# One core: a search for routing with one matmul per round less, transposes in threes, and a first expert in split halves, planned anew

## The chip, the core and the metric

The kernel runs on one core of a Trainium2 chip. The metric is device time in microseconds (us). A core has TensorE (matmuls; PE in the rows, and PEld for its weight loads), VectorE (DVE), ScalarE (ACT), GpSimd (POOL) and SyncE (SP); they run independently and wait for each other by semaphores. The working memory SBUF and the accumulation memory PSUM have 128 partitions; TensorE writes to PSUM only.

## The reference

Two parts. The first is a linear attention with a complex decay: for each of 4 x 8 heads and 768 positions, a state of 48 x 48 is multiplied by a normalised complex number per feature, the outer product of `k` and `v` is added to its real part, and `q` reads it.

```python
for t in range(S):
    new_re = ar * S_re - ai * S_im
    new_im = ar * S_im + ai * S_re
    S_re, S_im = (new_re + kv, new_im)
    y[:, :, t] = np.einsum('bhd,bhde->bhe', q[:, :, t], S_re)
```

The second is a mixture of eight experts with a capacity, on the 3072 tokens of 384 features that the first part gives.

```python
logits = x @ w_gate
order = np.argsort(-logits.flatten())
for idx in order:
    tok, e = (int(idx) // E, int(idx) % E)
    if assigned[tok] >= 0 or counts[e] >= cap:
        continue
    assigned[tok] = e
    counts[e] += 1
for e in range(E):
    mask = assigned == e
    out[mask] = np.maximum(x[mask] @ w1[e], 0.0) @ w2[e]
```

Each expert gets exactly 384 tokens, has a hidden width of 1024, and its weights are 384 x 1024 and 1024 x 384, all in fp32.

## The kernel before

**Attention** takes the first 223 us. It works on 24 chunks of 128 tokens; every engine has a part in it. GpSimd also builds the constants of the search there (`Router.masks`, `levels`, `level`, one call of `level` for each of five step sizes in `GRID`), between copies `gc` and `f` that attention needs.

**Routing** finds the experts one after another: whichever expert would be full first when tokens are taken in the order of their logits is settled, its tokens are taken out, and the rest is ranked again. `Router.find` does it by five rounds for each of the first seven experts. A round compares all keys with 32 thresholds (`ind`, VectorE), counts per expert how many keys are above each (`cnt`, six matmuls of bf16 on TensorE with `oh`), and moves the thresholds. As four columns of tokens go into one matmul, the counts come as four blocks, which have to be added: ScalarE copies the blocks into one column of a tile (`gather`, `comp`, four small ACTIVATEs), one matmul with the 0/1 matrix `sel` adds them, and VectorE subtracts what is needed (`cs`). VectorE then compares with zero and counts over the free axis (`f`, `fm`). Two matmuls add to the thresholds in PSUM (`thr`): one with `steps`, which needs no result, and one with `weight` and `fm`, which is the outcome of the round. The first search counts in another way (`by_pe`): 24 matmuls of which only one block is used.

From the outcome come the expert's number (`eidx`) and, by `slots`, the list of its 384 tokens (`idx`). GpSimd then starts the transfers of the expert's weights (`w1t`, `w2t`, 1.5 MB each) and of its tokens' rows (`xg`, three gathers). `update` ranks the rest.

**Experts.** `tokens` transposes the rows by nine fp32 matmuls of 128 x 128 (`acc<-ident,xg`). For experts 1 to 7 every fp32 factor is split into a high half, rounded by ScalarE (`w1h`, `xh`, `hh`, `w2h`), and the rest, taken by VectorE (`w1l`, `xl`, `hl`, `w2l`); a product is then three matmuls of 384 columns (`product`). Expert 0 (`WHOLE1`, `WHOLE2`) has no halves: one fp32 matmul a product, which stands as two records in the trace (`acc<-xh,w1t`, `acc<-w2t,hh`). There are 24 products in each of the two layers. Results are collected in five PSUM buffers named `acc`; a buffer of the first layer comes free when `hh` and `hl` have been made of it. Until the first expert's rows are there, `WARM` matmuls of constants keep TensorE running (`acc<-ident,mask`).

**The order** of everything from routing on is made by a planner on the host: `Plan` records the operations with a cost each, `rank` gives due times, moved by kind with the numbers in `M_OFF`, and `in_order` lists them for each engine. The engines run that list in order, so what waits at the head of an engine's queue holds up all that stands behind it. Nearly all instructions show line 135 (in the changed kernel 136), that of the helper that issues them, so rows are told apart by their tiles.

Of the kernel before, what the change touches and what calls it, by code (L numbers as in the profile page):

```python
# [37 lines left out]
SHUT = 8192.0  # L38
LEAD_R = 8
# [138 lines left out]
def in_order(ops, step, hop, wait, done_, start, slack, late=None):  # L178
# [25 lines left out]
    while len(done) < len(ops):  # L204
        pick = None
        for e, xs in ready.items():
            if xs:
                t = max(free[e], min(o.at for o in xs))
                o = min((o for o in xs if o.at <= t), key=lambda o: (o.prio, o.at, o.n))
                if slack and e == "dve":  # L210
                    h = min((o for o in xs if o.at <= t + 1.0), key=lambda o: (o.prio, o.at, o.n))
                    if h.prio < o.prio - 1500.0:
                        o = min((o for o in xs if o.at <= t and t + o.cost <= h.at + (0.05 if h.kind == "first" else slack)),
                                key=lambda o: (o.prio, o.at, o.n), default=h)
                t = max(t, o.at)
                if pick is None or t < pick[0]:
                    pick = t, o
        t, o = pick
        ready[o.eng].remove(o)
        cost = o.cost  # L220
        if o.eng == "pe":
            if not late_:
                cost = clock.take(t, cost, 0.84 if o.kind == "MX" else 1.0)
            elif o.main and t - busy > 3.4:
                cold = t
            if late_ and t < cold + 4.0:
                cost += min(cost, (cold + 4.0 - t) / 2)
            if o.main and side and t < run + 0.1:
                cost += BURST
            side, run = not o.main, t + cost  # L230
# [450 lines left out]
class Router:  # L681
# [27 lines left out]
    def levels(self, nc):  # L709
# [12 lines left out]
        jf = t("jf", [2, 32])  # L722
        g.iota(jf, pattern=[[1, 32]], base=0, channel_multiplier=0, allow_small_or_imprecise_dtypes=True)
        row = t("row", [2, 1])
        g.iota(row, pattern=[[0, 1]], base=0, channel_multiplier=1, allow_small_or_imprecise_dtypes=True)
        sa, sb = t("sa", [2, 32]), t("sb", [2, 32])
# [7 lines left out]
        for x in self.wide.values():  # L734
            for y in x:
                g.memset(y, 0.0)
        self.sel = t("sel", [128, 128], F16)
# [15 lines left out]
    def level(self, nc, i):  # L753
        v = g = nc.gpsimd
        jf, row, sa, sb = self.row
        d = GRID[i]
        nxt = GRID[i + 1] if i + 1 < len(GRID) else 0.0
        v.tensor_scalar(sa, jf, 1.0, -d, op0=OP.add, op1=OP.mult)
        v.tensor_scalar(sb, jf, nxt, None, op0=OP.mult)
        v.tensor_tensor(sb, sb, sa, op=OP.subtract)  # L760
        v.tensor_scalar(sb, sb, row, None, op0=OP.mult)
        v.tensor_tensor(self.steps[:2, i], sb, sa, op=OP.add)
        g.memset(self.weight[:, i], d)

    def start_plan(self, plan, wk, ps):
# [4 lines left out]
        self.wide = {n: [plan.wrap(y, BF if n == "f" else F32) for y in x] for n, x in self.wide.items()}  # L770

# [50 lines left out]
    def find(self, parts, by_pe, more):  # L822
# [16 lines left out]
        for it in range(len(GRID)):  # L839
# [131 lines left out]
    def update(self, more):  # L971
# [19 lines left out]
        v.scalar_tensor_tensor(need, e2, SHUT, cc, op0=OP.mult, op1=OP.subtract)  # L991
# [225 lines left out]
class Lane:  # L1217
# [3 lines left out]
    def __getattr__(self, name):  # L1221
        def call(*a, **k):
# [7 lines left out]
            else:  # L1230
# [3 lines left out]
                cost = n / rate / (2 if half else 1) + base  # L1234
                if self.e == "vector" and ("accum_out" in k or any(x.shape[1:] == [1] for x in ins[1:])):
                    cost += 0.06
# [26 lines left out]
def experts(nc, tc, z, router, w1, w2, xd, out):  # L1263
# [51 lines left out]
    def route(e):  # L1315
# [10 lines left out]
        rows(w1t.rearrange("p a f -> p (a f)"), w1, eidx, 128 * 3 * FF * 4, "w1d")  # L1326
        def second():
            w2t[e] = wp.tile([128, FK, DM], F32, name="w2t", bufs=2)
            rows(w2t[e].rearrange("p a f -> p (a f)"), w2, eidx, 128 * FK * DM * 4, "w2d")
# [6 lines left out]
        for j in range(3):  # L1336
            rows(xg[:, j], xd, i[:, j:j + 1], 128 * DM * 4, "xd")
# [9 lines left out]
        for kk in range(3) if e not in WHOLE1 else ():  # L1347
            split(w1t[:, kk], *(w[:, kk] for w in w1s[e]), "w1s", g if (e, kk) in W1_POOL else v)
# [7 lines left out]
    def tokens(e, xg):  # L1356
        xs = pair([128, 3, CAP], "x", 1) if e not in WHOLE1 else wp.tile([128, 3, CAP], F32R, name="xh", bufs=1)
        for kk in range(3):
            xp = pm.tile([128, 3, 128], F32, name="acc", bufs=5)
            for j in range(3):  # L1360
                o = plan.tensor.transpose(xp[:, j], xg[:, j, kk * 128:kk * 128 + 128], z.ident)
                o.main, o.kind = True, "tp"
            if e in WHOLE1:
                act(xs[:, kk].bitcast(F32), xp.rearrange("p a b -> p (a b)"), AF.Copy).kind = "x"
            else:
                split(xp.rearrange("p a b -> p (a b)"), *(x[:, kk] for x in xs), "x")
# [9 lines left out]
    for e in range(E):  # L1376
# [5 lines left out]
        for f in range(FK):  # L1382
# [6 lines left out]
            if whole2:  # L1389
                act(hs[:, f].bitcast(F32), hp, AF.Relu).kind = "h"  # L1390
                continue
            hi, lo = (h[:, f] for h in hs)
            act(hi, hp, AF.Relu).kind = "h"
            v.scalar_tensor_tensor(lo, hp, 0.0, hi.bitcast(F32), op0=OP.max, op1=OP.subtract).kind = "h"
            split(w2t[e][:, f], *(w[:, f] for w in w2s), "w2s", g if f in W2_POOL.get(e, ()) else v)
        for j in range(3):
# [7 lines left out]
            act(ot, op, AF.Copy).kind = "ot"  # L1404
# [7 lines left out]
            move(issue, [], [ot, idx[e][:, j:j + 1]], 128 * DM * 4, "out")  # L1412
# [17 lines left out]
M_STEP, M_HOP, M_WAIT, M_DONE, BURST = 0.11, 0.15, 0.56, 0.95, 0.0  # L1430
M_LATE = 0.0
M_OFF = {'find1': 835.4, 'find2': 177.3, 'find3': 5742.5, 'find4': 586.4, 'find5': 202.8, 'find6': -166.9, 'find7': 3964.4, 'first': 798.4, 'h': -267.8, 'mm': -1978.5, 'next0': -350.6, 'next1': 1725.6, 'next2': -434.0, 'next3': 1723.0, 'next4': 4459.0, 'next5': 3249.1, 'next6': 3238.8, 'ot': 399.1, 'out': 4151.6, 'slot1': 2379.8, 'slot2': 3913.1, 'slot3': 8365.8, 'slot4': -48.4, 'slot5': 45.4, 'slot6': 3905.5, 'slot7': 2159.9, 'tp': -5582.0, 'w1d': 5858.6, 'w1s': -1579.2, 'w2d': 1875.2, 'w2s': -466.1, 'warm': 426.7, 'x': 659.3, 'xd': 4044.8}
# [8 lines left out]
WHOLE1 = (0,)  # L1441
WHOLE2 = (0,)
# [49 lines left out]
```

## Time and profile before

| | |
|---|---|
| median of three timed runs | 499.46 us (499.0 to 499.57) |
| the profiled execution | 500.43 us, of which its span is 498.6 us |
| PE busy | 444.0 us (89%), 3644 matmuls |
| VectorE busy | 389.0 us (78%) |
| ScalarE busy | 305.6 us (61%) |
| GpSimd busy | 140.9 us (28%) |
| TensorE's granted clock, mean | 0.976 of full speed |

The rows that follow further down are in us from the start of the span. In the order of time each row has the start, how long it lasted, the engine, the operation with what it writes and reads, and how many follow each other (x6). Matmuls are pipelined: the duration of a row overlaps with its successors, and what one costs in a stream is the distance from start to start. A busy TensorE can therefore be slower than it has to be.

### The profile page before, as it was taken

To read this page: it belongs to the slowest core of one execution; us is meant where nothing else is said; L and a number is where in the kernel's file an instruction comes from. 1 tells how busy PE (TensorE), PEld (TensorE's weight loads), DVE (VectorE), ACT (ScalarE), POOL (GpSimd) and SP (SyncE) were. 2 spreads that over 40 slices of the span, in tenths; PEclk is the share of its full clock that TensorE was granted. 3 is DMA by queue.
4 is the path that set the end of the run, shared out by engine and by line. 5 is a ranking of instruction groups with operands and counts; after the bars stand their busy time and mean duration, and the time that the engine had idled before them with its cause. 6 is when DMAs were issued, how large, how long until landed. Compare 5 with 4: busy or idle time off the path is not lost.

```text
span 498.6 us, 9821 instructions
## 1 busy us (share of the span) xinstructions
PE 444.0 (89%) x3644; PEld 382.3 (77%) x3644; DVE 389.0 (78%) x1005; ACT 305.6 (61%) x577; POOL 140.9 (28%) x227
## 2 busy tenths in 40 slices
PE   0019999999999999995589999999999999999996
PEld 0006888888798998984465578888988888999995
DVE  5999999999999999736736878598996968925150
ACT  6999898989799859520033836374472843733241
POOL 5893020303031302121211314150321513830102
PEclk9999999999999999995599999999999999999999
DMA  7807876877897674620343415380360715650001
GB/s 236 333 11 208 269 242 214 263 228 236 265 302 182 224 199 128 186 63 34 143 158 141 177 50 173 143 307 10 96 255 32 286 49 224 267 175 16 33 16 49
DMA packets 37200, 82.52 MB, mean 165 GB/s; under 512 B 4352, under 2 KB 29184, under 8 KB 34080
## 3 DMA queue, kind: packets, MB, share of 16 engines
q1 hardware_dynamic: 29216, 41.96, 27.4%
q0 software_dynamic: 6848, 38.95, 21.3%
q10 hardware_dynamic: 1088, 0.98, 0.6%
q8 instruction: 29, 0.48, 0.4%
q14 instruction: 19, 0.16, 0.1%
HBM read 53.49 MB, written 9.44 MB: 126 GB/s over the span
## 4 chain that ended last, share of the span: by engine, by line
PE 71%; issue 14%; ACT 6%; DVE 3%; DMA 3%; POOL 2%; POOLq 1%; ACTq 0%; DVEq 0%
PE acc L135 29%; PE sc L135 14%; PE y L135 8%; PE U L135 8%; PE xp L135 4%; PE cnt L135 3%; PE kp L135 3%; ACT s L135 2%; DMA w1t<-in_w,eidx 2%; POOL out L135 2%; DMA ai<-in_a_im 1%; ACT L276 1%; ACT p L135 1%; DVE ind L135 1%; DVE f L135 1%
## 5 line engine op out<-in xcount | busy, mean ns | idle before, releaser
L135 ACT ACTIVATE hh<-acc 128x384 fp32r<-128x384 f32 (+1 forms) x64 | 31.3, 490 | 62.0 <-PE acc L135 54.1
L135 PE MATMUL sc<-mask,f 128*128 128x512 bf16 x111 | 29.3, 412 | 35.5 <-DVE f L135 35.5
L135 ACT ACTIVATE comp<-cnt 32x8 f16<-32x8 f32 (+1 forms) x144 | 24.2, 168 | 57.7 <-PE cnt L135 50.8
L135 PE MATMUL acc<-w2l,hh 128*128 128x384 f32 x168 | 56.7, 350 | 0.0
L135 PE MATMUL acc<-w2h,hl 128*128 128x384 f32 x168 | 56.3, 349 | 0.0
L135 PE MATMUL acc<-w2h,hh 128*128 128x384 f32 x168 | 55.3, 346 | 0.0
L135 PE MATMUL acc<-xh,w1h 128*128 128x384 f32 x168 | 55.1, 347 | 0.0
L135 PE MATMUL acc<-xh,w1l 128*128 128x384 f32 x168 | 54.8, 347 | 0.0
L135 PE MATMUL acc<-xl,w1h 128*128 128x384 f32 x168 | 54.5, 345 | 0.0
L135 POOL DMA_INDIRECT out<-ot,idx x24 | 24.3, 1012 | 106.5 <-ACT ot L135 97.0
L135 PEld LDWEIGHTS <-f 128*128 128x128 bf16 x111 | 10.8, 105 | 49.1 <-DVE f L135 35.5
L135 PE MATMUL sc<-KQ 96*128 96x128 f32 x384 | 48.1, 277 | 0.0
L135 DVE SCALAR_TENSOR_TENSOR hl<-acc,hh 128x384 fp32r<-128x384 f32 x56 | 30.6, 552 | 19.6 <-ACT hh L135 18.7
L135 PEld LDWEIGHTS sc<-KQ 96*128 96x128 f32 x384 | 45.1, 192 | 0.8 <-issue 0.7
L135 DVE TENSOR_TENSOR f<-kq,CS 128x1536 f32<-128x1536 f32 x24 | 41.6, 1750 | 1.0 <-ACT CS L135 0.5
L135 DVE TENSOR_TENSOR ind<-m,thr 128x768 bf16<-128x768 f32 (+1 forms) x45 | 33.9, 771 | 8.4 <-PE thr L135 8.4
L135 POOL DMA_DIRECT2D xd<-x x22 | 13.3, 604 | 93.6 <-ACT x L135 93.6
L135 POOL DMA_INDIRECT xg<-xd,idx x24 | 30.2, 1259 | 32.2 <-DVE idx L135 12.0
L135 DVE TENSOR_TENSOR am<-sc,mask 128x512 f32<-128x512 f32 x48 | 31.9, 680 | 6.8 <-PE sc L135 6.3
L135 PE MATMUL y<-am,V 128*64 128x128 f32 x384 | 36.5, 278 | 0.0
L135 PEld LDWEIGHTS acc<-w2l,hh 128*128 128x128 f32 x168 | 31.5, 189 | 0.7
L135 PEld LDWEIGHTS acc<-w2h,hl 128*128 128x128 f32 x168 | 31.3, 189 | 0.6 <-issue 0.3
(207 smaller groups left out, 1173.3 us busy)
## 6 DMA issues: line engine op xcount, KB each, us to landing
KQ<-f SPq DMA_DIRECT2D x144, 128.5 KB, 2.7
kq<-in_kq SPq DMA_DIRECT2D x8, 1152.0 KB, 6.8
V<-in_v SPq DMA_DIRECT2D x8, 576.0 KB, 5.3
xd<-x POOLq DMA_DIRECT2D x22, 192.0 KB
ar<-in_a_re SPq DMA_DIRECT2D x6, 576.0 KB, 4.1
ai<-in_a_im SPq DMA_DIRECT2D x6, 576.0 KB, 5.4
ar<-in_a_re SPq DMA_DIRECT2D x2, 384.0 KB, 4.8
ar<-in_a_re SPq DMA_DIRECT2D x2, 192.0 KB, 4.2
```

Of the source, the lines that this page charges most:

```text
L135: r = f(*a, **k)
L276: real.scalar.add_instruction(ins)
```

## The change

Five things are changed, all from routing on, but for constants that GpSimd builds in attention.

1. The rounds of `find` that are not `by_pe` (searches for experts 1 to 6, 30 rounds). ScalarE copies the four blocks to four slices of a tile `parts`, whose fifth slice holds the negated need, and one reduction on VectorE adds the five. The matmul with `sel` and the tile `comp` are gone here (the list in `slots` still uses them).
2. In the same rounds the `steps` matmul is merged into that with `fm`: the tile `fm` has ones in two spare rows (64 and 65), and `both` has the step there and the level in rows 0 to 31.
3. The three transposes of one block of features are one entry of the plan for experts 1 to 7, so they stand together.
4. `WHOLE1` and `WHOLE2` are empty: expert 0 is split like the others.
5. The planner has a cost `BURST` of 0.1 for a product behind a small matmul or a transpose, a floor for ScalarE's cost, kinds by expert, and new numbers in `M_OFF`.

```diff
-            nc.tensor.matmul(thr, z.onesb.to_broadcast([128, 128]), self.steps[:, it], start=False, stop=False, skip_group_check=True)
             if by_pe:
+                nc.tensor.matmul(thr, z.onesb.to_broadcast([128, 128]), self.steps[:, it], start=False, stop=False, skip_group_check=True)
                 nc.ops[-1].deps.append(counted)
...
             else:
-                nc.tensor.matmul(both[:, 1, :E], self.sel, self.gather(both, E), start=True, stop=True)
-                v.tensor_tensor(cnt, both[:32, 1, :E], need[:32], op=OP.subtract)
+                with nc.one():
+                    for c in range(4):
+                        nc.scalar.activation(self.parts[:, c], both[32 * c:32 * c + 32, 0, E * c:E * c + E], AF.Copy)
+                v.tensor_reduce(cnt, self.parts.rearrange("p c e -> p e c"), op=OP.add, axis=AX.X)
...
-            nc.tensor.matmul(thr, self.weight[:, it].to_broadcast([128, 128]), wide["fm"].bitcast(BF)[:, 1:2].to_broadcast([128, 32]),
-                             start=False, stop=(it == len(GRID) - 1), skip_group_check=True)
+            fmb = wide["fm"].bitcast(BF)[:, 1:2]
+            pair = (self.weight[:, it].to_broadcast([128, 128]), fmb.to_broadcast([128, 32])) if by_pe else (
+                fmb.to_broadcast([128, 128]), self.both[:, it])
+            nc.tensor.matmul(thr, *pair, start=False, stop=(it == len(GRID) - 1), skip_group_check=True)
...
-        v.scalar_tensor_tensor(need, e2, SHUT, cc, op0=OP.mult, op1=OP.subtract)
+        v.scalar_tensor_tensor(self.parts[:, 4], e2[:32], -SHUT, cc[:32], op0=OP.mult, op1=OP.add)
...
-        v.tensor_tensor(self.steps[:2, i], sb, sa, op=OP.add)
-        g.memset(self.weight[:, i], d)
+        g.tensor_tensor(self.both[r, i], sb, sa, op=OP.add)
+        g.tensor_copy(self.steps[r, i], self.both[r, i])
+        g.memset(self.both[:32, i], d)
+        g.memset(self.weight[:, i], 0.0)
+        g.memset(self.weight[:32, i], d)
...
-            for j in range(3):
-                o = plan.tensor.transpose(xp[:, j], xg[:, j, kk * 128:kk * 128 + 128], z.ident)
-                o.main, o.kind = True, "tp"
+            with plan.one() if e else nullcontext():
+                for j in range(3):
+                    o = plan.tensor.transpose(xp[:, j], xg[:, j, kk * 128:kk * 128 + 128], z.ident)
+                    o.main, o.kind = True, f"tp{e}"
...
-M_STEP, M_HOP, M_WAIT, M_DONE, BURST = 0.11, 0.15, 0.56, 0.95, 0.0
+M_STEP, M_HOP, M_WAIT, M_DONE, BURST = 0.11, 0.15, 0.56, 0.95, 0.1
...
-WHOLE1 = (0,)
-WHOLE2 = (0,)
+WHOLE1 = ()
+WHOLE2 = ()
```

**Where instructions stand.** TensorE, in the first expert: one round of the search for expert 1, from the last count (`cnt<-oh,ind`) to the outcome (`thr<-...fm`). Before:

```order
L135 LDWEIGHTS ind_2922
L135 MATMUL cnt<-oh,ind_2922 128x32
L135 LDWEIGHTS onesb
L135 MATMUL thr<-steps,onesb 128x32
L135 MATMUL acc<-xh,w1t 128x384 x2
L135 LDWEIGHTS sel
L135 MATMUL cnt<-comp_2935,sel 128x8
L135 MATMUL acc<-xh,w1t 128x384
L135 LDWEIGHTS weight
L135 MATMUL thr<-fm_183,weight 128x32
L135 MATMUL acc<-xh,w1t 128x384 x2
```

and now:

```order
L136 LDWEIGHTS ind_2920
L136 MATMUL cnt<-oh,ind_2920 128x32
L136 MATMUL acc<-xh,w1l 128x384
L136 MATMUL acc<-xl,w1h 128x384 x2
L136 MATMUL acc<-xh,w1h 128x384 x2
L136 MATMUL acc<-xh,w1l 128x384 x2
L136 MATMUL acc<-xl,w1h 128x384 x2
L136 LDWEIGHTS fm_184
L136 MATMUL thr<-both,fm_184 128x32
L136 MATMUL acc<-xh,w1h 128x384 x2
```

Between the counts and the outcome stand products alone, and the first expert's are of split halves.

VectorE, the same search for expert 1, rounds two to four (`cs` and `f,fm` are a round's outcome, `ind` the next comparison). Before:

```order
L135 TENSOR_TENSOR cs_187<-cnt,need 32x8
L135 TENSOR_SCALAR f_185,fm_183<-cs_187 32x8
L135 TENSOR_TENSOR ind_2883<-m,thr 128x768
L135 TENSOR_TENSOR cs_186<-cnt,need 32x8
L135 TENSOR_SCALAR f_184,fm_182<-cs_186 32x8
L135 TENSOR_TENSOR ind_2922<-m,thr 128x768
L135 TENSOR_TENSOR cs_187<-cnt,need 32x8
```

and now:

```order
L136 TENSOR_TENSOR w1l<-w1t,w1h 128x1024 x2
L136 TENSOR_REDUCE cs_189<-parts 32x8
L136 TENSOR_SCALAR f_187,fm_185<-cs_189 32x8
L136 TENSOR_TENSOR w1l<-w1t,w1h 128x1024
L136 TENSOR_TENSOR ind_2920<-m,thr 128x768
L136 TENSOR_TENSOR xl<-acc,xh 128x384 x3
L136 TENSOR_REDUCE cs_188<-parts 32x8
L136 TENSOR_SCALAR f_186,fm_184<-cs_188 32x8
L136 TENSOR_TENSOR ind_2957<-m,thr 128x768
L136 SCALAR_TENSOR_TENSOR hl<-acc,hh 128x384 x2
L136 TENSOR_REDUCE cs_189<-parts 32x8
```

The first expert's rests `w1l`, `xl` and `hl` stand between the steps of the search, where nothing stood.

TensorE, the transposes of expert 4's tokens among the second layer of expert 3. Before:

```order
L135 MATMUL acc<-ident,xg 128x128
L135 MATMUL acc<-w2h,hh 128x384
L135 MATMUL acc<-ident,xg 128x128
L135 MATMUL acc<-w2l,hh 128x384
L135 LDWEIGHTS weight
L135 MATMUL thr<-fm_183,weight 128x32
L135 MATMUL acc<-ident,xg 128x128
L135 MATMUL acc<-w2h,hl 128x384
L135 MATMUL acc<-ident,xg 128x128 x3
L135 MATMUL acc<-w2h,hh 128x384
```

and now, for expert 3's tokens:

```order
L136 MATMUL acc<-ident,xg 128x128 x3
L136 LDWEIGHTS fm_185
L136 MATMUL thr<-both,fm_185 128x32
L136 MATMUL acc<-w2l,hh 128x384
L136 MATMUL acc<-ident,xg 128x128 x3
L136 MATMUL acc<-w2h,hl 128x384
L136 MATMUL acc<-ident,xg 128x128 x3
```

The single transposes between products have become groups of three.

## Rows read from the trace of the kernel before

**Rows 1.** Stretches of 20 us: busy us of each engine (instructions), clock, DMA share.

```profile
240.00:260.00 20.00, 14.44 (x116) 11.50 (x116) 10.09 (x48) 4.43 (x20) 4.88 (x5) 0.76 0.54 188
260.00:280.00 20.00, 20.00 (x95) 11.58 (x94) 13.42 (x65) 9.41 (x27) 4.76 (x5) 1.00 0.48 187
380.00:400.00 20.00, 19.74 (x131) 17.59 (x130) 18.43 (x77) 12.02 (x35) 6.50 (x7) 1.00 0.54 202
```

**Rows 2.** PE in order of time: start, duration, operation.

```profile
296.95 0.33 PE L135 MATMUL acc<-xl,w1h 128*128 128x384 f32 x1
...
298.51 0.34 PE L135 MATMUL acc<-xl,w1h 128*128 128x384 f32 x1
...
298.99 0.34 PE L135 MATMUL acc<-xh,w1h 128*128 128x384 f32 x1
```

**Rows 3.** PE in order of time, first expert and start of the second.

```profile
255.61 0.91 PE L135 MATMUL acc<-xh,w1t 128*128 128x384 f32 x2 [0.35 <-ACT xh L135]
...
266.86 4.76 PE L135 MATMUL acc<-xh,w1t 128*128 128x384 f32 x14
271.45 0.42 PE L135 MATMUL cnt<-rh,o 128*128 128x96 bf16 x6
...
287.84 0.63 PE L135 MATMUL acc<-xh,w1h 128*128 128x384 f32 x1
```

**Rows 4.** PE in order of time, around small matmuls of the search for expert 3.

```profile
305.55 0.34 PE L135 MATMUL acc<-w2l,hh 128*128 128x384 f32 x1
...
306.02 0.33 PE L135 MATMUL acc<-w2h,hl 128*128 128x384 f32 x1
...
308.62 0.18 PE L135 MATMUL thr<-steps,onesb 128*128 128x32 bf16 x1
308.65 0.42 PE L135 MATMUL acc<-w2h,hh 128*128 128x384 f32 x1
...
309.25 0.33 PE L135 MATMUL acc<-w2h,hh 128*128 128x384 f32 x1
...
309.91 0.34 PE L135 MATMUL acc<-w2l,hh 128*128 128x384 f32 x1
```

**Rows 5.** PE in order of time, around transposes alone and in three.

```profile
315.17 0.27 PE L135 MATMUL acc<-ident,xg 128*128 128x128 f32 x1
...
315.46 0.27 PE L135 MATMUL acc<-ident,xg 128*128 128x128 f32 x1
...
378.31 0.49 PE L135 MATMUL acc<-ident,xg 128*128 128x128 f32 x3
378.56 0.42 PE L135 MATMUL acc<-w2h,hh 128*128 128x384 f32 x1
```

**Rows 6.** Three engines in order of time, one round of a search, and its list.

```profile
257.76 0.30 PE L135 MATMUL cnt<-oh,ind 128*128 128x32 bf16 x6
258.16 0.71 ACT L135 ACTIVATE comp<-cnt 32x8 f16<-32x8 f32 x4 [1.84 <-PE thr L135]
259.55 0.15 DVE L135 TENSOR_TENSOR cs<-cnt,need 32x8 f32<-32x8 f32 x1 [2.00 <-PE cnt L135]
260.07 0.18 PE L135 MATMUL thr<-fm,weight 128*128 128x32 bf16 x1
...
273.84 0.17 DVE L135 CAST idx<-at 128x3 int32<-128x3 f32 x1
```

**Rows 7.** VectorE's groups: times, busy us, mean ns of one, idle before.

```profile
L135 DVE SCALAR_TENSOR_TENSOR hl<-acc,hh 128x384 fp32r<-128x384 f32 x56 | 30.6, 552 | 19.6 <-ACT hh L135 18.7
L135 DVE TENSOR_TENSOR w2l<-w2t,w2h 128x384 fp32r<-128x384 f32 x56 | 29.0, 547 | 0.0
L135 DVE TENSOR_TENSOR w1l<-w1t,w1h 128x1024 fp32r<-128x1024 f32 x21 | 25.1, 1213 | 0.8 <-ACT w1h L135 0.8
```

**Rows 8.** GpSimd and VectorE in order of time, early in attention.

```profile
29.79 0.58 POOL L135 COPY f<-gc 128x6 f32<-128x6 f32 x2
33.65 5.20 DVE L135 TENSOR_TENSOR f<-kq,CS 128x1536 f32<-128x1536 f32 x3 [0.38 <-ACT CS L135]
```

More of the change, by code (lines that the diff above doesn't have):

```diff
@@ L1 @@
 import math
-from contextlib import ExitStack, contextmanager
+from contextlib import ExitStack, contextmanager, nullcontext
 import concourse.bass as bass
@@ L38 @@
 SHUT = 8192.0
+STEP_ROW = 64
 LEAD_R = 8
@@ L227, in in_order @@
                 cost += min(cost, (cold + 4.0 - t) / 2)
-            if o.main and side and t < run + 0.1:
+            small = not o.main or o.kind.startswith(("tp", "warm"))
+            if side and not small and t < run + 0.1:
                 cost += BURST
-            side, run = not o.main, t + cost
+            side, run = small, t + cost
             if o.main:
@@ L736, in levels @@
                 g.memset(y, 0.0)
+        for y in self.wide["fm"]:
+            g.memset(y[STEP_ROW:STEP_ROW + 2], 1.0)
+        self.parts = t("parts", [32, 5, E])
         self.sel = t("sel", [128, 128], F16)
@@ L753, in level @@
     def level(self, nc, i):
-        v = g = nc.gpsimd
-        jf, row, sa, sb = self.row
+        g = nc.gpsimd
+        r = slice(STEP_ROW, STEP_ROW + 2)
+        jf, row, sa, sb = (x[r] for x in self.row)
         d = GRID[i]
         nxt = GRID[i + 1] if i + 1 < len(GRID) else 0.0
[L758 to L761, printed above, removed]
-        v.tensor_tensor(self.steps[:2, i], sb, sa, op=OP.add)
-        g.memset(self.weight[:, i], d)
+        g.tensor_scalar(sa, jf, 1.0, -d, op0=OP.add, op1=OP.mult)
+        g.tensor_scalar(sb, jf, nxt, None, op0=OP.mult)
+        g.tensor_tensor(sb, sb, sa, op=OP.subtract)
+        g.tensor_scalar(sb, sb, row, None, op0=OP.mult)
+        g.tensor_tensor(self.both[r, i], sb, sa, op=OP.add)
[3 more added lines that the diff above has]
+        g.memset(self.weight[:32, i], d)
     def start_plan(self, plan, wk, ps):
@@ L770, in start_plan @@
         self.wide = {n: [plan.wrap(y, BF if n == "f" else F32) for y in x] for n, x in self.wide.items()}
+        self.parts = plan.wrap(self.parts)
     def mine(self, n, shape, dt=F32):
@@ L1234, in call @@
                 cost = n / rate / (2 if half else 1) + base
+                if self.e == "scalar":
+                    cost = max(cost, 0.18)
                 if self.e == "vector" and ("accum_out" in k or any(x.shape[1:] == [1] for x in ins[1:])):
@@ L1336, in route @@
         for j in range(3):
-            rows(xg[:, j], xd, i[:, j:j + 1], 128 * DM * 4, "xd")
+            rows(xg[:, j], xd, i[:, j:j + 1], 128 * DM * 4, f"xd{e}")
         if e in W2_LATE:
@@ L1347, in route @@
         for kk in range(3) if e not in WHOLE1 else ():
-            split(w1t[:, kk], *(w[:, kk] for w in w1s[e]), "w1s", g if (e, kk) in W1_POOL else v)
+            split(w1t[:, kk], *(w[:, kk] for w in w1s[e]), f"w1s{e}", g if (e, kk) in W1_POOL else v)
         plan.kind = f"next{e}"
@@ L1389, in experts @@
             if whole2:
-                act(hs[:, f].bitcast(F32), hp, AF.Relu).kind = "h"
+                act(hs[:, f].bitcast(F32), hp, AF.Relu).kind = f"h{e}"
                 continue
             hi, lo = (h[:, f] for h in hs)
-            act(hi, hp, AF.Relu).kind = "h"
-            v.scalar_tensor_tensor(lo, hp, 0.0, hi.bitcast(F32), op0=OP.max, op1=OP.subtract).kind = "h"
-            split(w2t[e][:, f], *(w[:, f] for w in w2s), "w2s", g if f in W2_POOL.get(e, ()) else v)
+            act(hi, hp, AF.Relu).kind = f"h{e}"
+            v.scalar_tensor_tensor(lo, hp, 0.0, hi.bitcast(F32), op0=OP.max, op1=OP.subtract).kind = f"h{e}"
+            split(w2t[e][:, f], *(w[:, f] for w in w2s), f"w2s{e}", g if f in W2_POOL.get(e, ()) else v)
         for j in range(3):
@@ L1411, in issue @@
                 scat.append(s)
-            move(issue, [], [ot, idx[e][:, j:j + 1]], 128 * DM * 4, "out")
+            move(issue, [], [ot, idx[e][:, j:j + 1]], 128 * DM * 4, f"out{e}")
             if j == 2 and e == E - 2:
```

22 lines of the change are left out of this document (12 added, 10 removed).

## The prediction

> **What bounds the kernel now.** I read the stretches first. From 260 us on TensorE is busy for 20.00 of 20 us in one stretch and 19.74 in another [rows 1], so the experts are bound by what TensorE issues, and each start that disappears from its queue is time off the end. VectorE beside it rises from 13.42 to 18.43 us of 20: a second engine that is not far from its own limit. Only in 240 to 260 us is TensorE not full (14.44 busy, granted clock 0.76, a mix of the levels 1.2 and 2.4 GHz) and VectorE half idle (10.09). Attention before that keeps its instructions on every engine but GpSimd.
>
> Then TensorE in order of time. In an undisturbed run nine products of 128x384 start between 296.95 and 298.51, so one takes 0.173 us [rows 2]. The 0.33 us that each row shows as duration overlaps with the next; what counts is the distance of the starts. The first expert's unsplit fp32 products cost two records each: fourteen records stand between 266.86 and 271.45, 0.328 each, 0.656 a product [rows 3].
>
> **Search rounds.** A small matmul in the stream costs more than its own turn, because the product behind it is followed late. Around a lone `sel` the starts go from 305.55 to 306.02, 0.47 for two products that alone take 0.35: 0.12 us. Where `sel` also waits for ScalarE's copy, 309.25 to 309.91, it is 0.31 [rows 4]. About one place in four is of the second kind, so I take 0.17. The `steps` matmul costs 0.03 (308.62 to 308.65) right behind the counts, and 0.48 less 0.35, 0.13, where it stands alone (298.51 to 298.99) [rows 2, 4]. Only seven of them stand alone in the order behind the first product; I take 0.05. The change removes both from each of 30 rounds. Ten rounds lie in the first expert's stretch, treated below as a whole. The 20 of the searches for experts 3 to 6 stand in a full stream: 20 x 0.22 = **-4.4 us**. The ends are 20 x 0.15 = 3.0 and 20 x 0.44 = 8.8. VectorE's subtraction becomes a sum over five parts on the same engine, and ScalarE still makes four copies; both cost nothing, since they take the place of an equal one.
>
> The Trainium skill, "TensorE: Matmul & The Clock Gate", section "Wait — 56ns, not 53.3ns?", has a floor of about 25 ns between starts, however small the matmul; two of them in 20 rounds would then bring an estimated 1.0 us instead of 4.4, and the result would be 3.4 us later. The start behind the small one agrees with that page (0.03), but the one after it comes late, and there the trace decides.
>
> **Grouped transposes.** Alone between products a transpose costs 315.17 to 315.46, 0.29 less 0.17: 0.12 us, three of them 0.36. Three in a row occupy 378.31 to 378.56, 0.25, and the product behind is followed 0.09 late: 0.34 [rows 5, 4]. Twenty-one groups of three thus gain at most 21 x 0.02 = 0.4 us. Many stood in runs already, so I take **-0.1**.
>
> **First expert.** Its 48 products at 0.656 (31.5 us) become 144 at 0.173 (24.9): -6.6 us of TensorE [rows 2, 3]. TensorE could also start earlier. Its first product now waits until 255.61 for `xh`, which stands behind a round's copies on ScalarE; in the new order `xh` comes before them, so I put the start at 254.1: -1.5.
>
> Both are kept only if the inputs of the next expert come earlier too. These are late results of the search for expert 1, whose list of tokens is ready at 273.84 [rows 6]; from there come the row gathers, the transposes and, at 287.84, its first product [rows 3]. VectorE carries this search, and the change puts in front of that list three `w1l` of 1.213, three `xl` and seven `hl` of about 0.55, and eight `w2l` of 0.547: 3.6 + 5.5 + 4.4 = 13.5 us [rows 7]. It had 9.9 + 6.6 us idle in the two stretches [rows 1], but in waits between rounds. The bounds are therefore 0 (all of it falls into waits) and +13.5 (none does). Walking both queues by hand with the durations of the rows, I find the list at about 276.9 instead of 273.84, 3 us later in spite of shorter rounds, and expert 1's first product at about 285.3 instead of 287.84. At that point the order leaves 23 split products of the first expert (4.0 us), where before five fp32 products were left (3.3 us). So the whole first stretch, its ten rounds included, is worth -2.5 + 0.7 = **-1.8 us**; in it TensorE stands still for some 4.5 us, at the closing counts and ranks of the search and longest, 1.6 us, at the counts of the list. The ends are -10.3 (6.6 + 1.5 + 10 x 0.22, no stall) and +3.2 (13.5 less 10.3, no cover at all).
>
> **Replanned order.** From a round's counts to its `fm` matmul something must happen that no order shortens: 257.76 to 258.16 until ScalarE starts, 0.71 for four copies, some 0.1 to VectorE, and 259.55 to 260.07 from there to `fm` [rows 6]: 1.7 us, ten products. The new order leaves 8 to 12 products there, where the old one had the time of `sel` as well. I add **+1.0** for such waits over the 20 rounds; 0 and +10 are the ends (below).
>
> **GpSimd** gets three more small instructions in each of the five levels and a few fills. Behind three levels stand its two copies into `f` for chunks 1 and 2, from 29.79 for 0.58 us; the stacking that reads them also waits for VectorE's rotation, which fills those tiles from 33.65 for 5.20 us [rows 8]. Chunk 1's turn ends at about 37.1. The nine instructions ahead of the copies have some 6.8 us before they are late, so I cost them at nothing; what they took above that would be added to the start of attention.
>
> **Sum.** -1.8 - 4.4 - 0.1 + 1.0 = -5.3 against the profiled execution: its own time is 500.43 (span 498.6 and what lies around it), so 495.1. The three timed runs have their median at 499.46, 0.97 lower, and I move the forecast by as much: **494.2 us**.
>
> **Rivals.** *No stall in the first expert.* If VectorE's extra work falls into its waits, the first stretch gives 10.3 instead of 1.8: about 485.7. For it: 16.5 us idle against 13.5 [rows 1, 7]. Against: the search runs on the same queue, in order. Chance 0.10.
>
> *The clock comes late.* The granted clock was 0.76 over 240 to 260 us [rows 1]: for some 9.6 us of it TensorE was at 1.2 GHz and rose while it ran multiplications of constants without pause. The new order mixes transposes into these, which wait for gathered rows. If TensorE is at 1.2 GHz for 6 us more, products take 0.35 instead of 0.17 there, and 3 us are lost: 497. Chance 0.10. The same page of the Trainium skill, section "Part 4: PE-mode transpose", says that transposes do not count as busy for the clock; by that rule this rival is the likely one. The old order ran nine transposes behind its warm-up and reached the higher level all the same, so the trace bears it out only in part.
>
> *Accumulators run out* (slower). Five `acc` buffers hold products until VectorE has made `hl`. In the new order only one or two of an expert's eight `hl` stand ahead of the next search's ranking; the rest come behind it. TensorE covers 5 x 9 x 0.173 = 7.8 us. If VectorE needs over that between freeing two buffers, TensorE stops in each expert: at 18.43 of 20 us busy [rows 1] there is little to give. A loss of 2 us in experts 1 to 5 each is +10: 504. It decides from about 1.1 us each, where the 5.3 are gone. Chance 0.12.
>
> *The rounds bring nothing.* If the search chain, not the number of starts, sets when TensorE goes on, the 4.4 us turn into waits at `fm`, and only the first stretch is left: 499, no difference. Against it: TensorE shows no wait of note behind 260 us. Chance 0.06.
>
> **Numbers.** The forecast case has 0.62, with 490 to 497 as its own range. Faster by over 0.2% (1.0 us, about what a measurement of this kernel can tell from no change): 0.62 + 0.10 + 0.10 = 0.82. Same 0.06. Slower 0.12. The range 487.5 to 499.0 leaves out the slower rival and most of the case without a stall, under 2 in 10.
>
> **What would show it.** Right: no `steps` or `sel` matmul in rounds; the first product of the first expert near 254 and expert 1's near 285; TensorE idle for about 4 us between 262 and 285, put down to VectorE; a period of about one us less for each of experts 2 to 5. Wrong: a granted clock below 1.00 after 256 us; waits of TensorE on `hl` in every expert; waits on `fm` that add up to several us; or a first expert without idle time.

## The result, and the profile after it

The changed kernel takes 492.17 us (median of four runs, 491.21 to 493.07) against 499.25 (four runs, 499.0 to 499.57): a ratio of 0.9853, with a 95% interval of 0.9835 to 0.9872. It is faster, as forecast, and 2.0 us faster than the 494.2 of the forecast. Two more groups of runs in the experiments give 492.36 against 498.91 and 493.75 against 500.0, 6.2 to 6.6 us apart instead of 7.1.

The profiled execution took 491.21 us with a span of 489.4, so it is 9.2 us below that of before (498.6) and the fastest of all runs of the changed kernel. The terms below are read from this pair. It overstates the gain: the profiled execution of before lay 1.2 us above the median of its four runs, that of the changed kernel 1.0 below. The other runs of the changed kernel lie 0.8 to 3 us above it, and not always for one reason: of the two that were profiled too (`again` and `again2`, below), one has its first routing matmul at 228.94 instead of 226.56, the other loses 1.3 us behind 291 us, half of it in a wait for ScalarE's copy `ot`.

The stretches of 20 us, with the columns of [rows 1]:

```profile
240.00:260.00 20.00, 14.06 (x124) 12.61 (x125) 16.56 (x65) 7.40 (x23) 5.91 (x5) 0.77 0.52 188
260.00:280.00 20.00, 18.82 (x126) 16.02 (x124) 17.85 (x80) 10.49 (x35) 4.91 (x6) 1.00 0.44 177
380.00:400.00 20.00, 20.00 (x145) 18.08 (x144) 17.02 (x43) 14.36 (x46) 4.42 (x5) 1.00 0.47 190
```

VectorE has 4.4 to 6.5 us more in the two stretches of the first expert, and TensorE is no longer full in the second: 18.82 instead of 20.00. Behind that TensorE is full again.

TensorE in order of time, as [rows 3] and [rows 5]: the first routing matmul, the first product, the counts of the list, the next expert's first product, and the last one of all:

```profile
226.56 0.19 PE L136 MATMUL thr<-start,onesb 128*128 128x32 bf16 x1 [0.98 <-ACT x L136]
...
254.68 0.44 PE L136 MATMUL acc<-xh,w1h 128*128 128x384 f32 x1 [0.36 <-ACT xh L136]
...
273.12 0.43 PE L136 MATMUL cnt<-rh,o 128*128 128x96 bf16 x6 [0.99 <-DVE rh L136]
...
283.42 0.44 PE L136 MATMUL acc<-xh,w1h 128*128 128x384 f32 x1
...
484.26 0.34 PE L136 MATMUL acc<-w2h,hl 128*128 128x384 f32 x1
```

In the kernel before, the last product stands at 493.48 and the first routing matmul at 224.96:

```profile
224.96 0.19 PE L135 MATMUL thr<-start,onesb 128*128 128x32 bf16 x1 [0.97 <-ACT x L135]
```

So routing began 1.60 us **later** than before (226.56 to 224.96), and the first product came 0.93 earlier all the same (255.61 [rows 3] to 254.68): routing itself took 2.5 us less. Of these, 2.35 lie between the issue of the first row gather and the first product: 9.12 us before (246.49 to 255.61), 6.77 now (247.91 to 254.68).

The waits of TensorE's matmuls from 253 us to the end, so with the last transposes ahead of the first product, by engine and what it waited for: us, times, longest.

```profile
PE cnt L136 <- DVE rh L136: 1.0, 1, 1.0
PE acc L136 <- ACT xh L136: 0.4, 1, 0.4
PE acc L136 <- DMA xg<-xd,idx: 0.3, 1, 0.3
PE cnt L136 <- DVE ind L136: 0.2, 1, 0.2
```

Only one is above 0.4 us, and none is on `hl` or `fm`. But a matmul also waits through the load of its weights, and for `fm` and for a buffer that `hl` sets free it does so there:

```profile
PEld L136 <- DVE f L136: 2.4, 11, 0.4
PEld acc L136 <- DVE hl L136: 1.1, 4, 0.4
```

These are small: the load for a small matmul stands 0.16 us idle at almost every place, whatever it waits for, and only three of the eleven are above that (0.45, 0.43 and 0.25). The four for `hl` are 0.38, 0.29, 0.26 and 0.19.

A round of the search for expert 3, from the outcome to the next counts and the outcome after that:

```profile
302.26 0.34 PE L136 MATMUL acc<-xh,w1l 128*128 128x384 f32 x1
302.44 0.19 PE L136 MATMUL thr<-both,fm 128*128 128x32 bf16 x1
302.48 0.42 PE L136 MATMUL acc<-w2l,hh 128*128 128x384 f32 x1
302.74 0.34 PE L136 MATMUL acc<-xl,w1h 128*128 128x384 f32 x1
...
303.78 0.32 PE L136 MATMUL cnt<-oh,ind 128*128 128x32 bf16 x6
303.95 0.60 PE L136 MATMUL acc<-w2h,hl 128*128 128x384 f32 x2
```

Between 302.26 and 302.74 lie two products, 0.35 us, and the outcome, which costs 0.13 as before. Neither `sel` nor `steps` stands in the round any more: that is two matmuls less per round, not the one of the title.

**The ledger.** From the starts of all matmuls between the first product and the last I took off 0.1736 us for each of the products of 128x384 (the distance of starts in runs of products alone, 0.173 to 0.174) and 0.656 for each unsplit one. What is left is small matmuls and waits. I cut it where the search for expert 2 closes (its `thr<-start`, 293.89 before and 291.18 after).

| part, in the profiled executions | forecast | measured |
|---|---|---|
| attention, up to the first routing matmul | 0 | +1.6 |
| routing, to the first product | -1.5 | -2.5 |
| first expert: 48 x 0.656 = 31.5 to 144 x 0.1736 = 25.0 | -6.6 | -6.5 |
| small matmuls and waits up to the cut: 5.4 to 8.9 | +6.3 | +3.5 |
| the same behind the cut: 26.2 to 20.9 | -3.5 | -5.3 |
| sum | -5.3 | -9.2 |

(The forecast's first stretch was -1.8; with -1.5 and -6.6 in it, +6.3 was left for small matmuls and waits. Its -3.5 is -4.4 - 0.1 + 1.0.)

### The profile page after: what moved, and what is told of

Its sections match the earlier page's. It is cut to its first block, busy times and chain, and to the rows that moved or that the text cites. A ratio compares the mean times of both kernels' runs of the same rounds, so it can differ in the third digit from the quotient of the medians.

```text
span 489.4 us, 9869 instructions
## 1 busy us (share of the span) xinstructions
PE 431.8 (88%) x3632; PEld 386.0 (79%) x3632; DVE 401.4 (82%) x1027; ACT 311.4 (64%) x588; POOL 141.1 (29%) x245
## 4 chain that ended last, share of the span: by engine, by line
PE 66%; issue 12%; POOL 6%; DVE 5%; DMA 5%; ACT 3%; SPq 2%; POOLq 1%; ACTq 0%; DVEq 0%
PE acc L136 27%; PE sc L136 12%; PE y L136 8%; PE U L136 7%; PE xp L136 4%; PE cnt L136 3%; DMA w1t<-in_w,eidx 3%; PE kp L136 3%; SPq L136 2%; POOL sb L136 2%; DMA pick<-in_w_gate 1%; ACT w1h L136 1%; DVE ind L136 1%; POOL sel L136 1%; POOL out L136 1%
## 5 line engine op out<-in xcount | busy, mean ns | idle before, releaser
L136 PE MATMUL acc<-xh,w1h 128*128 128x384 f32 x192 | 62.5, 344 | 0.4 <-ACT xh L136 0.4
L136 PE MATMUL acc<-xh,w1l 128*128 128x384 f32 x192 | 62.0, 341 | 0.0
L136 PE MATMUL acc<-xl,w1h 128*128 128x384 f32 x192 | 61.7, 341 | 0.0
L136 PE MATMUL acc<-w2h,hl 128*128 128x384 f32 x192 | 61.4, 344 | 0.0
L136 PE MATMUL acc<-w2h,hh 128*128 128x384 f32 x192 | 61.3, 344 | 0.0
L136 ACT ACTIVATE hh<-acc 128x384 fp32r<-128x384 f32 x64 | 30.2, 492 | 35.9 <-PE acc L136 35.5
L136 ACT ACTIVATE parts<-cnt 32x8 f32<-32x8 f32 x120 | 20.1, 168 | 44.2 <-PE cnt L136 41.7
L136 PEld LDWEIGHTS acc<-xh,w1h 128*128 128x128 f32 x192 | 35.6, 189 | 1.8 <-DVE hl L136 0.8
L136 PEld LDWEIGHTS acc<-xl,w1h 128*128 128x128 f32 x192 | 35.8, 189 | 0.2
L136 PEld LDWEIGHTS acc<-w2h,hh 128*128 128x128 f32 x192 | 35.6, 188 | 0.4 <-DVE hl L136 0.3
```

Of the source, the lines that this page charges most:

```text
L136: r = f(*a, **k)
```

## Why attention starts later

ScalarE and GpSimd in order of time, near 30 us, in the kernel before (ScalarE, then GpSimd):

```profile
28.95 1.28 ACT L276 ACT_TABLE_LOAD   x1
30.25 1.16 ACT L135 ACTIVATE s<-ai 128x1152 f32<-128x1152 f32 x1
```

```profile
29.44 0.29 POOL L135 COPY gc<-s 128x6 f32<-128x6 f32 x1
```

and in the changed kernel:

```profile
28.27 1.28 ACT L278 ACT_TABLE_LOAD   x1
32.31 1.16 ACT L136 ACTIVATE s<-ai 128x1152 f32<-128x1152 f32 x1 [2.76 <-POOL gc L136]
```

```profile
20.07 1.42 POOL L136 TENSOR_SCALAR sb<-jf 2x32 f32<-2x32 f32 x1
...
29.74 0.33 POOL L136 TENSOR_SCALAR sb<-jf 2x32 f32<-2x32 f32 x1
...
32.09 0.19 POOL L136 COPY gc<-s 128x6 f32<-128x6 f32 x1
```

ScalarE's square writes into a tile that GpSimd's copy `gc` must have read. Before, `gc` ended at 29.73, half a microsecond ahead of the end of ScalarE's table load at 30.23. Now it stands behind nine more instructions, ScalarE waits 2.76 us for it, and TensorE's first matmul of attention comes at 37.53 instead of 35.51:

```profile
35.51 4.88 PE L135 MATMUL sc<-mask,f 128*128 128x512 bf16 x11 [35.51 <-DVE f L135]
```

```profile
37.53 2.74 PE L136 MATMUL sc<-mask,f 128*128 128x512 bf16 x6 [37.53 <-DVE f L136]
```

The three levels ahead of `gc` took 12.35 us (19.74 to 32.09), and 9.91 before (19.53 to 29.44): 2.4 more. Most of that is the nine instructions themselves: from the sum `both` of the third level to `gc` are 0.93 us (31.16 to 32.09), where before the sum `steps` and `gc` lay 0.22 apart (29.22 to 29.44), so 0.7 a level.

In both kernels the levels also lasted longer than their instructions alone would. The same instruction `sb<-jf` took 0.33 us at 29.74 and 1.42 at 20.07, where VectorE ran a sum of two tiles of SBUF:

```profile
19.98 1.34 DVE L136 TENSOR_TENSOR s<-s,s 128x1152 f32<-128x1152 f32 x1
```

The Trainium skill, "SBUF — State Buffer", section "SBUF: two separate sides", says that VectorE, in an operation with two inputs in SBUF, and a GpSimd operation that reads SBUF exclude each other for a whole instruction. The rows agree: 20.07 plus 1.42 is 21.49, just behind the end of VectorE's at 21.32.

Three runs test it. In late_const only the fills and copies that nothing in attention needs were moved behind the last level:

```diff
         g.tensor_tensor(self.both[r, i], sb, sa, op=OP.add)
-        g.tensor_copy(self.steps[r, i], self.both[r, i])
-        g.memset(self.both[:32, i], d)
-        g.memset(self.weight[:, i], 0.0)
-        g.memset(self.weight[:32, i], d)
+        if i < len(GRID) - 1:
+            return
+        g.tensor_copy(self.steps[r], self.both[r])
+        g.memset(self.weight, 0.0)
+        for n, x in enumerate(GRID):
+            g.memset(self.both[:32, n], x)
+            g.memset(self.weight[:32, n], x)
```

> GpSimd builds the parts of the new constants that no step of attention needs (the copy to steps, the fills of both and weight) behind the last of the five levels instead of within each. Theory: in the changed kernel the copy gc stands behind three longer levels and holds ScalarE's square for 2.76 us, so attention starts 1.7 us late; then gc comes near 29.0 us, TensorE's first matmul near 35.5 us instead of 37.5, and the time is 490.4 us. Rival: the late start comes from transfers or the spread of the start, not from GpSimd's queue; then TensorE's first matmul stays near 37.5 us and the time near 492.2.

Beside it ran the unaltered kernel:

> The changed kernel once more, unaltered, to see how its profile and its median stand to each other. Expected: 492.2 us within 0.5, and first count matmul of attention near 37.5 us again. If the first profile (491.21) was the typical one and the three later runs were disturbed, the median comes out near 491.2.

Measured: 490.38 us (489.65 to 493.77), the unaltered kernel 492.36 (492.0 to 493.24), both against 498.91. That is 2.0 less, as the theory has it. The rows went only half the way: in the profile of late_const `gc` comes at 31.38 and not near 29.0, ScalarE still waits 0.88 for it (3.54 in the control), and TensorE's first matmul is at 36.84, the control's at 38.20. That execution is the slowest of its five, for a reason given at the end. The unaltered kernel's median is near the one of its first group, so the first profiled execution is the fastest and not the typical one.

late_all moves all that only the search needs, so also masks that the kernel before had in front of `gc`:

```diff
+    def rest_of(self, nc):
...
+        g.tensor_copy(self.steps[r], self.both[r])
...
-        parts = [self.masks, self.levels] + [lambda nc, i=i: self.level(nc, i) for i in range(len(GRID))]
+        parts = [self.masks, self.levels] + [lambda nc, i=i: self.level(nc, i) for i in range(len(GRID))] + [self.rest_of]
...
-    op(("later", n), "pool", LATER[n], NT - 1.0, lambda fn=fn: fn(nc), [("later", n - 1)])
+    op(("later", n), "pool", LATER[n], NT - 1.0, lambda fn=fn: fn(nc), [("later", n - 1)] + ([("P0", 5)] if n == 7 else []))
```

> As late_const, but everything that only the search needs (sel, the masks of the list, the fills) is built behind the copies of the third group of chunks, where GpSimd has some 25 us free. Theory: ScalarE no longer waits for gc at all (0.88 us were left in late_const, 2.8 to 3.5 in the changed kernel), TensorE's first matmul comes near 35.2 us, and the time is 489.6 us. Rival: gc is not what holds the start; then 492.3 us.

This first run had no changed kernel beside it, and came to 494.34 (493.1 to 496.11) against 500.08: not what was expected, although TensorE's first matmul was at 35.83 and the first product at 253.49. So it was repeated with a control on the same chip.

> late_all again, now beside the changed kernel on the same chip. Theory (GpSimd's longer constants hold ScalarE's square, and with it attention): 2 us less than the control, 1.5 to 2.5, TensorE's first matmul 2 us earlier. Rival (what is gained at the start is lost again behind it): within 0.7 us of the control.

> The changed kernel unaltered, as a control for the three runs beside it on the same chip: 492 to 496 us, 1.2 to 1.5% below the kernel before.

Measured: 490.72 (490.31 to 491.72) against 493.75 (492.3 to 494.15) of the control, 3.0 less; the profiles are 1.6 apart (spans 488.9 and 490.5). ScalarE in late_all_b, then in the control:

```profile
28.16 1.28 ACT L278 ACT_TABLE_LOAD   x1
29.45 1.16 ACT L136 ACTIVATE s<-ai 128x1152 f32<-128x1152 f32 x1
```

```profile
29.43 1.28 ACT L278 ACT_TABLE_LOAD   x1
31.52 1.16 ACT L136 ACTIVATE s<-ai 128x1152 f32<-128x1152 f32 x1 [0.81 <-POOL gc L136]
```

The wait is gone, and TensorE's first matmul moves from 36.74 to 34.68. Of these 2.06 us only 0.81 is the wait: ScalarE's table load came 1.27 earlier, and it varies as much in the unaltered kernel (28.27, 28.16 and 29.43 in its three profiles). Over all profiles, ScalarE waits 2.76, 3.54 and 0.81 for `gc` in the changed kernel and TensorE starts at 37.53, 38.20 and 36.74; in late_all and late_all_b it does not wait at all, and TensorE starts at 35.83 and 34.68. With both medians below that of their control, this shows that the late start was in GpSimd's queue. How much of the 3.0 is what the change added, and how much the older masks, was not separated. late_all_b beats both kernels, with a ratio of 0.9821 to before (0.9799 to 0.9844). What the first run of late_all lost again lies behind the start: in its profile TensorE waits 1.17 us for `ind` at the third counts of the search for expert 2, where late_all_b and the control wait 0.26 and 0.25, and the second expert's `w1h` starts 9.6 us after its transfer was issued instead of 9.3. Why transfers were slower in that group of runs was not tried. The two groups show how far a median can be trusted: one kernel, late_all, has 494.34 in one and 490.72 in the other on the same chip, while the kernel before has 500.08 and 500.0. A difference of 3 us between two kernels counts only beside a control in the same group, with rows that show where it is.

## What a small matmul costs

The forecast gave 0.12 us to a small matmul that stands alone and 0.03 to one behind another. Three kernels add 56 or 60 matmuls of constants (128x8, bf16) to the 20 rounds behind the cut, at places picked when the list is issued, so that the order of all else stays:

```diff
+    def small(to):
+        nc.tensor.matmul(to.real(), z.onesb.to_broadcast([128, 128]), router.start[:, :8], start=True, stop=True)
...
+            if main and left and run >= 2:
+                small(to)
+                left, run = left - 1, 0
```

That is lone60; behind60 calls `small` three times directly behind the counts, and lone_free is lone60, with 60 of them, with the output in a tile of the bank `sm` instead of the counts' bank.

> In the 20 rounds of the searches for experts 3 to 6, 56 more matmuls of constants (128x8, bf16, nothing waits for them), each alone between products, at least two products apart. Theory (a lone small matmul costs 0.12 to 0.13 us, as read around sel): 56 x 0.13 = 7.3 us more, 499.5 us. Rival (the floor between starts, 0.025): 1.4 us more, 493.6.

> The same matmuls of constants, three in each of the 20 rounds, but directly behind the counts. Theory (a small matmul right behind another costs only 0.03): 60 x 0.03 = 1.8 us more, 494.0 us. Rival (each start of a small matmul costs 0.12 wherever it stands): 7.2 us more, 499.4.

Measured: behind60 493.27 us (492.88 to 494.2), 0.9 above the control's 492.36. Lone60 509.29, 16.9 above: over twice the theory. Its profile has a cause that I had not meant to put in: 19 of the 56 wait for ScalarE's copies out of the same bank, 8.3 us in all. The first of them:

```profile
301.78 0.17 PE L136 MATMUL cnt<-start,onesb 128*128 128x8 bf16 x1 [0.45 <-ACT parts L136]
```

> lone60 again with the outputs in a bank that no other engine reads at that time, so that none of the 60 matmuls of constants waits for ScalarE. Theory (a lone small matmul costs 0.13 us): 60 x 0.13 = 7.8 us more than the changed kernel, 500.1 us. Rival (the floor between starts, 0.025): 493.8. If the 17 us of lone60 came from standing alone and not from waits, 509 again.

Measured: 501.67 us (500.82 to 503.71). That group had no control; the one of the next group on that chip is 7.9 lower (493.75). The rows are surer: in the ledger of lone_free the 60 matmuls take 7.8 us, 0.13 each, and none waits. TensorE there, in order of time:

```profile
306.78 0.18 PE L136 MATMUL sm<-start,onesb 128*128 128x8 bf16 x1
306.82 0.59 PE L136 MATMUL acc<-w2h,hh 128*128 128x384 f32 x2
307.25 0.18 PE L136 MATMUL sm<-start,onesb 128*128 128x8 bf16 x1
```

and in behind60, the three behind the counts:

```profile
305.31 0.32 PE L136 MATMUL cnt<-oh,ind 128*128 128x32 bf16 x6
305.48 0.22 PE L136 MATMUL cnt<-start,onesb 128*128 128x8 bf16 x3
305.55 0.59 PE L136 MATMUL acc<-w2h,hl 128*128 128x384 f32 x2
```

From 306.78 to 307.25 are 0.47 us for two products of together 0.35: one alone costs 0.12. Behind the counts three cost 0.07, the distance of counts and product having grown from 0.17 (303.78 to 303.95) to 0.24: 0.02 each. The Trainium skill's floor ("TensorE: Matmul & The Clock Gate", section "Wait — 56ns, not 53.3ns?", about 25 ns between starts) agrees with the second and not with the first; by the floor alone lone_free would have been near 495, an estimate. Why the product behind a lone small matmul is followed late, by its own weight load or by the change from bf16 to fp32, was not tried. And lone60 shows the third price: a small matmul that comes before its input or its bank is free costs that wait as well, as `sel` did [rows 4].

old_rounds undoes parts 1 and 2 of the change, and leaves the plan's numbers:

```diff
-                with nc.one():
-                    for c in range(4):
-                        nc.scalar.activation(self.parts[:, c], both[32 * c:32 * c + 32, 0, E * c:E * c + E], AF.Copy)
-                v.tensor_reduce(cnt, self.parts.rearrange("p c e -> p e c"), op=OP.add, axis=AX.X)
+                nc.tensor.matmul(both[:, 1, :E], self.sel, self.gather(both, E), start=True, stop=True)
+                v.tensor_tensor(cnt, both[:32, 1, :E], need[:32], op=OP.subtract)
```

> The changed kernel with the old rounds (sel and steps as matmuls of their own, the subtraction on VectorE), planned anew with the changed kernel's numbers. Theory (the starts are what the rounds gave): the 20 steady rounds lose 5.0 us, the ten of the first expert up to 2 more, 497.3 to 499.3 us. Rival (the new order of the work gave it): within 1 us of 492.3.

Measured: 514.32 us (512.52 to 515.92), 15 above what the theory had and far from the rival. Part of it is the rounds: by the ledger, small matmuls and waits between the closings of the searches for experts 2 and 5 take 16.9 us instead of the control's 13.2, 3.7 over 15 rounds. The two starts alone are 3.0 of it, from start to start 1.9 us for the fifteen `sel` and 1.1 for the `steps`, 0.20 a round; a wait of 0.46 for gathered rows is in the remainder. The rest of the 15 us lies outside these rounds, in waits that the other operations did not have in this order, and in and behind the longest of them (4.2 us, to 471.5) the granted clock was 0.50 from 470 to 480:

```profile
PE acc L136 <- DMA xg<-xd,idx: 7.6, 4, 4.2
PE cnt L136 <- DVE ind L136: 2.1, 4, 1.0
```

So the total of old_rounds tells nothing of the rounds' worth; the rows do, with 0.20 a round against the 0.22 of the forecast. In this order no `sel` waited for ScalarE and each cost 0.12 to 0.13; in the kernel before most of them waited (below). What a `sel` costs depends on the order.

## What the split of the first expert is worth, and the order

whole_held keeps the changed kernel's order and takes the split out: two of each three products are left out and the third becomes one fp32 product; `w1h`, `w1l`, `xl`, `hl`, `w2h`, `w2l` of this expert are not made.

```diff
+                if single:
+                    a, b = single[i // 3]
+                    p.fn = nothing if i % 3 < 2 else lambda a=a, b=b, i=i: nc.tensor.matmul(
+                        o.real(), a.real(), b.real(), start=(i == 2), stop=(i == n - 1))
```

> The changed kernel with its order of the work kept, but the first expert unsplit: of each three products one fp32 product is left in the last one's place, and w1h, w1l, xl, hl, w2h, w2l of this expert are left out. Theory (split halves save 6.5 us of products and give back 2 to 2.8 in TensorE's waits for VectorE): 3.7 to 4.5 us above the control. Rival (the waits pay all of it back): within 1 us of the control. Were nothing paid back, 6.5 us above it.

Measured: 497.49 us (496.09 to 498.07), 3.7 above the control's 493.75. In its ledger, products take 6.5 us more and everything else up to the cut 3.3 less (5.4 instead of 8.6). So the split is worth 6.5 us of TensorE, and 3.3 of them come back in the same stretch. One us of the 3.3 is shown to be a wait for VectorE: the control waits 1.01 at the counts of the list, whole_held, without the first expert's rests, not at all. A lone small matmul also costs 0.10 between unsplit products and 0.13 between split ones; how the rest divides was not tried.

Would less of that work on VectorE help? w2_pool is late_all with four of the first expert's eight `w2l` on GpSimd:

```diff
-W2_POOL = {}
+W2_POOL = {0: (0, 2, 4, 6)}
```

> As late_all, and four of the eight w2l of the first expert are taken by GpSimd instead of VectorE, planned anew. Theory (VectorE's extra work in the first expert is what makes TensorE stand still there): 4 x 0.55 = 2.2 us less in front of the list for the second expert, stalls shorter by about 1 us: 488.6 us. Rival (the search's own chain sets the stalls, and GpSimd's rests come late): 489.6 us or up to 2 us more.

Measured: 494.32 us (493.17 to 496.13), beside late_all's 494.34 in that group: no difference. The theory fell for this order. GpSimd took 4.55 us for the four, 1.14 each against VectorE's 0.55 [rows 7], and the new order puts the stalls elsewhere: TensorE's largest are now on a round's outcome and on `ind`.

```profile
267.41 0.19 PE L136 MATMUL thr<-both,fm 128*128 128x32 bf16 x1 [1.33 <-DVE f L136]
...
283.44 0.32 PE L136 MATMUL cnt<-oh,ind 128*128 128x32 bf16 x6 [1.05 <-DVE ind L136]
```

Last, the changed operations in a new order, made by the planner with the numbers of before:

```diff
-M_STEP, M_HOP, M_WAIT, M_DONE, BURST = 0.11, 0.15, 0.56, 0.95, 0.1
+M_STEP, M_HOP, M_WAIT, M_DONE, BURST = 0.11, 0.15, 0.56, 0.95, 0.0
```

and `M_OFF` as before.

> The changed kernel's operations with the planner's numbers of the kernel before (BURST 0, the old offsets). Theory (the removed starts and the split are worth their time in any sensible order): within 2 us of the control. Rival (the order has to be fitted to the operations, as old_rounds suggests from the other side): 5 us or more above the control, in waits of TensorE for tokens or for search results.

Measured: 500.36 us (498.7 to 501.97), 6.6 above the control and no faster than the kernel before (ratio 1.0003, 0.9987 to 1.0018). Stretches of old_plan, with the columns of [rows 1], and TensorE there:

```profile
280.00:290.00 10.00, 3.34 (x31) 2.63 (x31) 7.09 (x17) 5.86 (x18) 4.13 (x4) 0.67 0.60 231
290.00:300.00 10.00, 10.00 (x57) 8.96 (x56) 7.99 (x47) 1.16 (x5) 0.96 (x1) 0.82 0.16 46
```

```profile
279.07 0.42 PE L136 MATMUL acc<-w2h,hl 128*128 128x384 f32 x1
280.27 0.32 PE L136 MATMUL cnt<-oh,ind 128*128 128x32 bf16 x6 [0.78 <-DVE ind L136]
281.86 0.19 PE L136 MATMUL thr<-both,fm 128*128 128x32 bf16 x1 [1.28 <-DVE f L136]
...
287.69 0.34 PE L136 MATMUL cnt<-oh,ind 128*128 128x32 bf16 x6 [1.79 <-DVE ind L136]
...
290.36 0.52 PE L136 MATMUL acc<-w2l,hh 128*128 128x384 f32 x1
290.84 0.34 PE L136 MATMUL cnt<-oh,ind 128*128 128x32 bf16 x6
```

TensorE runs out of the first expert's products at 279, has only the search's own matmuls until the second expert's tokens come at 288, and then runs at 1.2 GHz (granted clock 0.50 from 284 to 293): from 290.36 a product takes 0.32 to 0.48 to the next start. The five waits for `ind` and `f` between 279 and 288 are 7.2 us, as much as the whole change gained (7.1).

## Why the prediction was right, and where it was off

- **Products and small matmuls.** 0.173 a product, 6.5 us for the split, 0.12 for one alone and 0.02 to 0.03 behind another: all as read from [rows 2 to 4], and shown again by lone_free, behind60 and whole_held. For the 20 rounds the forecast took 4.4 us, at 0.22 each, and that was too little. From start to start in the trace of before, the 20 `sel` cost 4.8 us, 0.24 each and not 0.17: 13 of the 20 cost over 0.2, where the forecast had one place in four wait. With 0.8 for the `steps` the two starts cost 5.6, 0.28 a round.
- **Replanned order.** "I add +1.0 for such waits over the 20 rounds" was too much: the 20 matmuls with `fm` cost 2.3 us before and 2.7 now (2.4 and 2.9 in the two other profiles), so such waits are 0.1 to 0.6 us. The 54 transposes behind the cut cost about 6.7 before and 6.5 to 6.8 now; the -0.1 of the forecast cannot be told from nothing. With these terms, -5.6 + 0.4 - 0.1, the part behind the cut comes to -5.3 as the ledger has it, where the forecast had -3.5.
- **First expert.** Walking the queues by hand was near at its beginning and late towards its end: the list was forecast at 276.9 and came at 275.62, expert 1's first product at 285.3 and came at 283.42.

```profile
275.62 0.16 DVE L136 CAST idx<-at 128x3 int32<-128x3 f32 x1
```

  The 4.5 us of standing still were mis-sized. The longest wait, at the counts of the list, was 1.15 us from start to start where 1.6 was forecast; with those at the first and third counts (0.3 and 0.4), a round's outcome (0.3) and a buffer (0.2), some 2.4 us in all. The rest of the 3.5 us up to the cut is not in more small matmuls, for there are 80 of them instead of 88; a lone one costs 0.13 instead of 0.10, and the remainder is many small delays that I did not divide.
- **GpSimd.** "I cost them at nothing" is the step that failed: 1.6 us in the profiles, 2.0 in the medians of late_const and its control. I had looked at the copies `f`, which have room to spare [rows 8], and not at `gc` in front of them, for which ScalarE waits. It hid behind the other errors, nearly all of which made the forecast too slow.
- **The sum.** In the profiles the terms missed by +1.6, -1.0, -2.8 and -1.8, and the gain was 9.2 us instead of 5.3; in the medians it was 7.1. That the forecast of 494.2 lay no more than 2.0 us off is in part luck: one error stood against the others.
- **Rivals.** Accumulators: four short waits for `hl`, 1.1 us in all, although VectorE is busy for 17.0 to 19.0 of 20 us up to 420 us. The rounds brought what was claimed and more. The clock did not come late, but the order did not put that rival to the test: the granted clock rose from 0.50 to 1.00 near 249 us, as before near 249.7, and the first transpose stood at 251.23, behind the rise. In the kernel before the transposes stood behind it too (253.25), so the prediction's argument that it rose in spite of them does not hold. That a gap brings the lower level back is a real danger, which old_plan shows with the same operations.

## What to carry to other kernels

Price a small matmul by where it stands: alone in a stream of large ones it cost 0.12 to 0.13 us here, behind another small one 0.02, and if its input is not there yet, the wait as well. Look for its waits at the weight loads too. When an idle engine is given more work, look up every instruction queued behind it and who waits for that, not only the one you know. Where the order of work is planned by fitted numbers, operations and order are one change: in an order made with the old numbers the same operations were worth nothing.

## What the runs showed that was not expected

In late_const the granted clock fell inside attention, where TensorE had waited 1.40 us for a transfer: from 64 to 68 us it was 0.59, 1.00 in the changed kernel, and this run ended at 493.77 where the others of this kernel were at 489.65 to 491.87.

```profile
64.64 0.84 PE L136 MATMUL kp<-ident,KQ 96*128 96x96 f32 x4 [1.40 <-DMA KQ<-f]
```

```profile
64.00:68.00 4.00, 3.36 (x22) 2.54 (x24) 3.96 (x10) 2.48 (x3) 0.00 (x0) 0.59 0.64 172
```

One late transfer cost twice: set against the changed kernel instruction by instruction, TensorE lost 1.6 us in this wait and 1.6 more by the slower clock behind it. It need not: in `again` the same transfer was late too, and the granted clock stayed at 1.00 from 62 to 70 us.

```profile
65.96 0.52 PE L136 MATMUL kp<-ident,KQ 96*128 96x96 f32 x4 [1.50 <-DMA KQ<-f]
```

Why the transfer was late, and why the clock fell in one run and not in the other, was not tried.
